# A new order of all steps in a layer of dilated window attention and gated MLP, with GpSimd's spreads of chunk 2 placed ahead of chunk 1's second norm

## The chip, the cores and the metric

The kernel runs on one core of a Trainium2 chip. The metric is the device time of one execution in microseconds (us), as the median of several. The engines have these names in the profile: PE is TensorE (matmuls; PEld its weight loads), DVE is VectorE, ACT is ScalarE, POOL is GpSimd and SP is SyncE, which only issues DMAs here. "L571" is line 571 of the kernel.

## What is computed

One block of a transformer over 2048 rows of 512 numbers in bfloat16. A layernorm, then attention with 32 heads of 16 in which each position sees itself and seven earlier ones at a distance of 2; then a second layernorm, and a gated MLP of width 1376 with a ReLU gate. Both halves add to their input.

```python
x = A_x
h = x + attention(_layernorm(x), A_wqkv, A_wo)     # W, dil = 8, 2; softmax over 8 offsets
n = _layernorm(h)
gate, up = n @ W_gate, n @ W_up
h2 = h + ((gate * (gate > 0)) * up) @ W_down
```

## The kernel before

The 2048 rows are worked in four chunks of 512, numbered 0 to 3 (`tk` in the code), and each chunk runs through the same steps.

- **First norm.** VectorE takes mean and variance (L492, L495), the rows are scaled (L548 to L553) and transposed, on TensorE with the identity (L582) or, for chunk 3, by a DMA transpose on SyncE's queue (L571).
- **q, k, v.** Twelve groups of four matmuls (L623), each written to one of the eight PSUM banks and copied out by ScalarE (L631).
- **Scores.** VectorE multiplies q with eight shifted copies of k (L674, in chunk 0 L689; L718 adds two products in some places), and TensorE sums over each head's numbers with the 0/1 matrix `sel` (L680, L732). There are two score groups for each chunk, for offsets 0 to 3 and 4 to 7 (`hf`), and ScalarE takes the exponential (L760). A sum of both halves goes through TensorE (L777) for the denominator, and VectorE multiplies each half with the reciprocal (L804).
- **Spreads.** The weights of a half lie on 32 partitions per offset. Four DMAs spread them to all 128 partitions (L820). A table, `BCD`, says which queue issues them: SyncE for most, GpSimd for the second half of chunk 2, the first half of chunk 3 and a part of chunk 0.
- **Weighted sum of v.** VectorE multiplies with shifted copies of v (L852, L867), half of the sum is done by accumulating DMAs that GpSimd issues (L895), and the rest by VectorE (L855, L859, L889).
- **Output projection and second norm.** Four groups of four matmuls (L933); VectorE adds the residual and sums the row (L944), centres it (L546; in chunk 0 ScalarE does it, L544), and SyncE transposes it by DMA (L571). The factor one over the standard deviation is applied only at the end. ScalarE sums the squares for it (L482).
- **MLP.** Gate and up groups of four matmuls (L1010), a narrow last one (L973), ReLU and copy on ScalarE (L1015, L1017, L1020), their product on VectorE (L1041; the narrow one L986 or L988, transposed by L996), then the down projection (L1064) and the output (L1070 or L1072). In chunks 0 and 1 the residual is added by an accumulating DMA of GpSimd (L1093).

What sets the order: each step is an operation with an engine, a planned duration, its dependences and its buffers. A planner goes through all 751 operations by a table of ranks, `RANK`, gives each the next free time of its engine, and the program is recorded in that order. So the table decides the order on every engine, and which of the buffers (five large ones of eight times 512, nine "quads" of transposed rows, eight banks) a step gets. Each engine works through its own row of instructions in that order and waits where an input isn't ready. SyncE's DMAs go out in their order as well. The two W_up loads (L317) wait for the attention of chunk 0, since their place is still used until then.

The operation of a spread is recorded like this; the line of its planned duration is the one that the change edits beside the table:

```python
abd.append(add(("bd%d%s" % (hf, eng[0]), tk), eng, len(ws) * BDI[eng[0]] + (0.35 if tk == 0 else 0), f_bd, [exd[hf]], apr + 1,
```

Of the kernel before, what the change touches and what calls it, by code (L numbers as in the profile page):

```python
# [15 lines left out]


RANK = [
# [38 lines left out]
]  # L57


# [34 lines left out]
class Plan:  # L94
# [9 lines left out]
    def add(self, key, *a, **k):  # L104
        op = Op(*a, **k)
        op.key = key
        op.seq = len(self.ops)
        if RANK:
            op.prio = RANK[op.seq]
        self.ops.append(op)  # L110
        for b in set(op.take) | set(op.use):
            b.left += 1
        return op
# [88 lines left out]
def kernel(  # L202
# [164 lines left out]
    add = plan.add  # L367
# [20 lines left out]
    BDI = {"S": 0.63, "A": 0.65, "P": 0.95}  # L388
# [217 lines left out]
    for tk in range(NCK):  # L606
# [48 lines left out]
        apr = base + 20  # L655
        exs, exd = [], []
# [3 lines left out]
        for hf in range(2):  # L660
            sc, ex = Buf(at_s), Buf(ex_s)
            scd, prd = [], []
            for t in range(0, NT, 2):
# [32 lines left out]
                else:  # L696
                    a = add(("pr%d" % hf, tk), "DVE", D40, f_pr, [d[k] for k in (t, t + 1) for d in (qd, kd, kp)],
                            apr, take=[pb], use=[qT], lat=DL)
# [110 lines left out]
        ab, abd = Buf(ab_s), []  # L809
        for w0 in range(0, W, BCN):  # L810
            hf = w0 // 4
            if (tk, hf) in BCD:
                for eng, q in (("SP", nc.sync), ("ACT", nc.scalar), ("POOL", nc.gpsimd)):
                    ws = [w for w in range(4) if BCD[tk, hf][w] == eng[0]]
                    if not ws:
                        continue

                    def f_bd(ws=ws, q=q, w0=w0, ab=ab, ex=exs[hf]):
                        for w in ws:
                            q.dma_start(ab.t[:, w0 + w, :], ex.t[w * HB:(w + 1) * HB, :].unsqueeze(1).to_broadcast([HB, 4, CS]))  # L820

                    abd.append(add(("bd%d%s" % (hf, eng[0]), tk), eng, len(ws) * BDI[eng[0]] + (0.35 if tk == 0 else 0), f_bd, [exd[hf]], apr + 1,
                                   take=[ab], use=[exs[hf]], lat=0.92 + ((-0.2 if hf == 0 else 0.6) if tk == 0 else 0),
                                   dq=(1.38 - BDI[eng[0]] * len(ws), 0.5 + BDI[eng[0]] * (len(ws) - 1))))
                continue
            bcs = [Buf(at_s) for _ in range(BCN)]

            def f_bc(w0=w0, bcs=bcs, ex=exs[hf]):
                for n, bc in enumerate(bcs):
                    r = (w0 + n) % 4 * HB  # L830
                    nc.tensor.matmul(bc.t[:], lhsT=spread[r:r + HB, :], rhs=ex.t[r:r + HB, :],
                                     start=True, stop=True, tile_position=(r, 0))

            a = add(("bc%d" % hf, tk), "PE", MM + SW, f_bc, [exd[hf]], apr + 1, take=bcs, use=[exs[hf]], lat=PEL)
            for n, bc in enumerate(bcs):
                def f_be(w=w0 + n, bc=bc, ab=ab):
                    nc.scalar.copy(out=ab.t[:, w, :], in_=bc.t[:])

                abd.append(add(("be%d" % hf, tk), "ACT", A5, f_be, [a], apr + 1, take=[ab], use=[bc], lat=AL))
# [120 lines left out]
        for f0 in range(0, NFT, 2):  # L960
# [42 lines left out]
            for ft in fts:  # L1003
# [31 lines left out]
                d = add(("ge%d" % (f0 // 2), tk), "ACT", A5, f_ge, [c], pr - 200, take=[gr], use=[gm], lat=AL)  # L1035
# [118 lines left out]
```

## Time and profile before

| what | value |
|---|---|
| median of 3 runs | 192.62 us (192.37 to 193.03) |
| profiled execution, its own time | 193.05 us |
| its span, from the first to the last instruction | 191.3 us |
| DMA transposes of the second norm (L571), chunk 1 | issued from 87.26 us, over 5.13 us |
| GpSimd's spreads (L820), chunk 2, second half | issued from 91.29 us, over 2.23 us |
| TensorE's wait ahead of chunk 1's MLP | 1.52 us, up to 95.72 us |

How to read it. A timeline row gives the start, the length, the engine, the line, the operation, what it writes and reads, and how many instructions were merged into it; behind it in brackets stands the idle time of the engine ahead of the row and what ended it. "SPq" rows are DMAs being issued; "DMA to landing" counts from the issue of a DMA to its last byte. A row of the waits is: engine and line, what it waited for, total, times, longest. In the chain of waits a row gives the start, the length and the step. By groups, a row gives busy time and the mean ns of one instruction behind the bar. A row of windows gives the stretch, its length, and the busy time of PE, PEld, DVE, ACT and POOL, each with a count, then the clock, the DMA share and GB/s.

### The profile page before, as it was taken

How to read it: one execution, taken by the hardware profiler on the slowest of the kernel's cores; microseconds unless marked ns; L12 is line 12 of the kernel's file. 1: busy time of each engine (PE TensorE's matmuls, PEld its weight loads, DVE VectorE, ACT ScalarE, POOL GpSimd, SP SyncE). 2: the span in 40 equal slices, each digit the busy share in tenths (PEclk: the TensorE clock that was granted, in tenths of full speed). 3: DMA queues.
4: the chain of work that ended last, by engine and by line, in shares of the span. 5: the costliest groups of instructions: out<-in, count | busy, mean ns of one | idle time of the engine just before them, and what ended most of it. 6: DMA issues, size and time to landing. Idle time of an engine off the chain costs nothing.

```text
span 191.3 us, 2948 instructions
## 1 busy us (share of the span) xinstructions
PE 183.1 (96%) x1058; PEld 92.3 (48%) x1077; DVE 149.3 (78%) x226; ACT 116.4 (61%) x241; POOL 25.1 (13%) x46
## 2 busy tenths in 40 slices
PE   7799998999999999999799999999999999999994
PEld 7555454554454435544244455444455446444453
DVE  6899989999999999999997979899382905022233
ACT  4579997986784585784428885132758612369600
POOL 3000403300000032100514214013300000000000
PEclk9999999999999999999999999999999999999999
DMA  5799384990598979862736899969930342201002
GB/s 183 267 326 386 76 206 94 194 202 17 178 209 188 280 167 188 153 137 55 160 63 124 165 192 213 152 151 178 179 54 3 92 100 82 55 3 55 0 24 86
DMA packets 27742, 26.96 MB, mean 141 GB/s; under 512 B 14704, under 2 KB 23248, under 8 KB 27728
## 3 DMA queue, kind: packets, MB, share of 16 engines
q1 hardware_dynamic: 23696, 15.47, 31.2%
q0 software_dynamic: 3312, 10.49, 28.5%
q10 hardware_dynamic: 720, 0.82, 1.3%
q8 instruction: 8, 0.13, 0.3%
q14 instruction: 6, 0.05, 0.1%
HBM read 8.42 MB, written 2.10 MB: 55 GB/s over the span
## 4 chain that ended last, share of the span: by engine, by line
PE 78%; DVE 8%; DMA 6%; ACT 4%; issue 2%; SPq 1%; DVEq 0%; ACTq 0%
PE bank L1010 35%; PE bank L1064 20%; PE bank L623 11%; PE bank L933 7%; DVE big L689 4%; DMA x_sm<-in_A_x_dram 3%; PE bank L973 3%; DMA big<-ex 3%; DVE st L492 2%; PE bank L680 2%; ACT up_sb L1015 1%; DVE big L867 1%; ACT quad L631 1%; PE bank L582 1%; PE bank L732 1%
## 5 line engine op out<-in xcount | busy, mean ns | idle before, releaser
L1010 PE MATMUL bank<-quad,wgu_sb 128*128 128x512 bf16 x312 | 70.6, 379 | 1.9 <-issue 1.5
L1010 PEld LDWEIGHTS <-wgu_sb 128*128 128x128 bf16 x320 | 30.9, 98 | 39.4 <-issue 3.3
L1064 PE MATMUL bank<-wd_sb,gT 128*128 128x512 bf16 (+3 forms) x195 | 39.1, 355 | 0.2
L623 PE MATMUL bank<-quad,wqk_sb 128*128 128x512 bf16 (+1 forms) x131 | 30.0, 370 | 0.6 <-DMA wqk_sb<-in_A_wqkv_dram 0.5
L1041 DVE TENSOR_TENSOR gT<-gr,up_sb 128x1024 bf16<-128x1024 bf16 x20 | 13.7, 690 | 20.7 <-ACT gr L1020 16.8
L1020 ACT ACTIVATE gr<-bank 128x512 bf16<-128x512 f32 x40 | 23.3, 605 | 9.0 <-PE bank L1010 9.0
L1064 PEld LDWEIGHTS <-gT 128*128 128x128 bf16 (+1 forms) x198 | 18.5, 98 | 19.4
L674 DVE TENSOR_TENSOR big<-quad,kT 128x4096 bf16<-128x4096 bf16 x11 | 25.0, 2285 | 0.0
L1017 ACT CAST up_sb<-bank 128x512 bf16<-128x512 f32 x30 | 17.1, 594 | 10.8 <-PE bank L1010 5.1
L623 PEld LDWEIGHTS <-wqk_sb 128*128 128x128 bf16 x134 | 14.7, 114 | 13.3 <-DMA wqk_sb<-in_A_wqkv_dram 1.1
L852 DVE TENSOR_TENSOR big<-big,vT 128x4096 bf16<-128x4096 bf16 x9 | 20.6, 2288 | 0.0
L482 ACT ACTIVATE junk<-x_sm,sm 128x512 bf16<-128x512 bf16 x17 | 12.3, 726 | 8.1 <-DVE x_sm L944 8.1
L623 PE MATMUL bank<-quad,wv_sb 128*128 128x512 bf16 x62 | 15.9, 379 | 0.1
L895 POOL DMA_DIRECT2D big<-big x13 | 11.2, 869 | 35.7 <-DVE big L852 25.5
L933 PE MATMUL bank<-wo_sb,quad 128*128 128x512 bf16 x61 | 14.5, 379 | 0.1
L1072 DVE SCALAR_TENSOR_TENSOR row<-bank,iv,x_sm 128x512 bf16<-128x512 f32 (+2 forms) x10 | 6.2, 641 | 10.6 <-issue 5.6
L855 DVE TENSOR_TENSOR big<-big 128x1024 bf16<-128x1024 bf16 (+1 forms) x17 | 10.4, 624 | 2.3 <-DMA big<-big 2.3
L820 POOL DMA_DIRECT2D big<-ex x12 | 6.8, 592 | 38.2 <-DVE st L492 19.0
L631 ACT CAST kT<-bank 128x512 bf16<-128x512 f32 x16 | 9.2, 592 | 4.0 <-PE bank L623 3.1
L944 DVE SCALAR_TENSOR_TENSOR x_sm<-x_sm,bank 128x512 bf16<-128x512 bf16 x16 | 10.7, 678 | 0.6 <-PE bank L933 0.6
L631 ACT CAST quad<-bank 128x512 bf16<-128x512 f32 x16 | 9.1, 590 | 2.7 <-PE bank L623 2.7
L492 DVE BATCH_NORM_STATS2 st<-x_sm 128x6 f32<-128x512 bf16 x15 | 9.7, 680 | 0.8 <-DMA x_sm<-in_A_x_dram 0.8
(84 smaller groups left out, 184.4 us busy)
## 6 DMA issues: line engine op xcount, KB each, us to landing
big<-big POOLq DMA_DIRECT2D x13, 512.0 KB, 5.0
big<-ex SPq DMA_DIRECT2D x20, 128.0 KB, 2.7
big<-ex POOLq DMA_DIRECT2D x12, 128.0 KB, 4.1
wgu_sb<-in_B_W_gate_dram SPq DMA_DIRECT2D x1, 1376.0 KB, 9.7
wgu_sb<-in_B_W_up_dram SPq DMA_DIRECT2D x2, 688.0 KB, 5.8
wd_sb<-in_B_W_down_dram SPq DMA_DIRECT2D x2, 640.0 KB, 5.5
x_sm<-in_A_x_dram SPq DMA_DIRECT2D x2, 512.0 KB, 6.4
wqk_sb<-wqk_sb POOLq DMA_DIRECT2D x2, 512.0 KB, 5.3
```

The source lines that it names most:

```text
L482: nc.scalar.activation(out=junk[:, j % 2, :], in_=h.t[:] if h else x_sm[:, tk * BPC + j, :], func=ACT.Square, bias=sm.t[:, j:j + 1], scale ...
L492: V.bn_stats(out=st.t[:], in_=x_sm[:, tk * BPC + j, :])
L623: nc.tensor.matmul(mm.t[:, lo:hi], lhsT=wv_sb[:, dt, t:D:NT] if c == 2 else wqk_sb[:, dt, c * D + t:(c + 1) * D:NT], rhs=xnT.t[:, dt, lo:h ...
L631: nc.scalar.copy(out=o, in_=mm.t[:])
L674: V.tensor_tensor(out=pb.t[:].rearrange("p (t w) s -> p t w s", t=2), in0=q4, in1=k4, op=ALU.mult)
L852: V.tensor_tensor(out=mt.t[:], in0=ab.t[:], in1=v8, op=ALU.mult)
L933: nc.tensor.matmul(od.t[:], lhsT=OT.t[:, t, j * P:(j + 1) * P], rhs=wo_sb[:, t, :], start=(t == 0), stop=(t == NT - 1 and tk not in RPE))
L1010: nc.tensor.matmul(mm.t[:fs, lo:hi], lhsT=wgu_sb[:, dt, g, ft * P: ft * P + fs], rhs=hnT.t[:, dt, lo:hi], start=(dt == 0), stop=(dt == NT ...
L1017: nc.scalar.copy(out=ub.t[:fs, i, :], in_=um.t[:fs, :])
L1020: nc.scalar.activation(out=gr.t[:fs, i, :], in_=gm.t[:fs, :], func=ACT.Relu, scale=-1.0 if tk in HX else 1.0)
L1041: V.tensor_tensor(out=gt.t[:fs, 0:n, :], in0=gr.t[:fs, 0:n, :], in1=ub.t[:fs, 0:n, :], op=ALU.mult)
L1064: nc.tensor.matmul(od.t[:, c0:c1], lhsT=gts[ft].t[:fs, ft % 2, j * P:(j + 1) * P], rhs=wd_sb[:fs, ft, c0:c1], start=(ft == 0), stop=(ft == ...
```

## The change

It edits two things. The table `RANK` is replaced: 751 other ranks. And the planned duration of GpSimd's spread of the first half in chunk 0 is raised from 0.35 to 0.85 above its base; this number enters the plan and no instruction.

```diff
 RANK = [
-    0, 1, 2, 3, 5, 6, 7, 8, 14, 15, 13, 12, 16, 17, 18, 19, 20, 21, 4, 9,
+    1, 0, 2, 3, 5, 8, 9, 11, 14, 15, 12, 13, 17, 16, 18, 19, 20, 21, 4, 7,
...
-                    abd.append(add(("bd%d%s" % (hf, eng[0]), tk), eng, len(ws) * BDI[eng[0]] + (0.35 if tk == 0 else 0), f_bd, [exd[hf]], apr + 1,
+                    abd.append(add(("bd%d%s" % (hf, eng[0]), tk), eng, len(ws) * BDI[eng[0]] + ((0.85 if eng=="POOL" and hf==0 else 0.35) if tk == 0 else 0), f_bd, [exd[hf]], apr + 1,
```

The instructions are the same in number and kind on every engine; only their order and their buffers differ. Three places follow. In each, the numbers behind a name are those of the buffers, and they differ between the two orders without a meaning of their own.

**VectorE, second norm of chunk 1, before.** `ex` is the weights of a half of chunk 2, `x_sm` the rows with the residual, `row` the centred rows.

```order
L944 SCALAR_TENSOR_TENSOR x_sm,sm_123<-x_sm,bank_140 128x512
L1041 TENSOR_TENSOR gT_98<-gr_111,up_sb_109 128x1024
L546 TENSOR_SCALAR row_108<-x_sm,sm_123 128x512
L804 TENSOR_TENSOR ex_101<-ex_101,rec_103 128x512
L718 TENSOR_TENSOR big_91<-big_91,wqk_sb 128x4096
```

The multiply L804, on whose result GpSimd's spreads of chunk 2 wait, stands behind the last of the four L546.

**VectorE, the same place now**, from that multiply to the first residual addition L944 of chunk 1.

```order
L804 TENSOR_TENSOR ex_100<-ex_100,rec_103 128x512
L674 TENSOR_TENSOR big_88<-quad_87,kT 128x4096
L986 SCALAR_TENSOR_TENSOR row_108<-gr_112,bank_144 128x2x96
L855 TENSOR_TENSOR big_91<-big_91 128x1024
L855 TENSOR_TENSOR big_92<-big_92 128x1024
L889 TENSOR_TENSOR quad_79<-big_91 128x512
L889 TENSOR_TENSOR quad_79<-big_92 128x512
L674 TENSOR_TENSOR big_89<-quad_87,kT 128x4096
L944 SCALAR_TENSOR_TENSOR x_sm,sm_123<-x_sm,bank_140 128x512
L546 TENSOR_SCALAR row_105<-x_sm,sm_123 128x512
```

It has moved ahead of all four L944 and L546. GpSimd's own row keeps the four spreads at the same place, behind the four accumulating DMAs of chunk 1.

**SyncE, second norm of chunk 0, before**, from the loads of W_up to the first spreads of chunk 1.

```order
L317 DMA wgu_sb<-in_B_W_up_dram 128x2x1376 x2
L571 DMA_TRANSPOSE quad_80<-row_106 128x4x128
L571 DMA_TRANSPOSE quad_80<-row_107 128x4x128
L571 DMA_TRANSPOSE quad_80<-row_104 128x4x128
L571 DMA_TRANSPOSE quad_80<-row_105 128x4x128
L820 DMA big_89<-ex_100 128x1x512 x4
```

**SyncE, the same place now.**

```order
L317 DMA wgu_sb<-in_B_W_up_dram 128x2x1376
L571 DMA_TRANSPOSE quad_80<-row_106 128x4x128
L317 DMA wgu_sb<-in_B_W_up_dram 128x2x1376
L571 DMA_TRANSPOSE quad_80<-row_105 128x4x128
L571 DMA_TRANSPOSE quad_80<-row_107 128x4x128
L571 DMA_TRANSPOSE quad_80<-row_104 128x4x128
L820 DMA big_90<-ex_100 128x1x512 x4
```

The first transpose now goes out between the two loads.

**TensorE, ahead of the second score group of chunk 1, before.** Two rows, a weight load and a matmul, stand for each matmul; the last matmul and the first of the scores are shown.

```order
L623 MATMUL bank_146<-quad_84,wqk_sb 128x512
L933 LDWEIGHTS quad_85
L933 MATMUL bank_147<-wo_sb,quad_85 128x512
...
L680 LDWEIGHTS sel
L680 MATMUL bank_145<-big_90,sel 32x512
```

**TensorE, the same place now.**

```order
L933 MATMUL bank_143<-wo_sb,quad_85 128x512
L933 LDWEIGHTS quad_85
L933 MATMUL bank_142<-wo_sb,quad_85 128x512
...
L680 LDWEIGHTS sel
L680 MATMUL bank_144<-big_88,sel 32x512
```

In both orders the first score group of chunk 1 begins at row 609 of TensorE. The second begins at row 705 before and at row 697 now: between the two groups stand 32 matmuls before (eight groups of four) and 28 now (seven). The first gate or up matmul of chunk 1 is at row 1174 in both, so that the four matmuls now stand behind the scores. The first L1010 of chunk 0 is at row 795 before and 787 now.

In chunk 2, VectorE's product L852 that stood behind the gate product L1041 stands ahead of it now.

74 rows, old and new, of the table RANK are left out of this document.

## The prediction

> **What bounds the kernel now.** I read the page first: busy time by engine, the granted clock, the shares of the chain.
>
> ```profile
> span 191.3 us, 2948 instructions
> PE 183.1 (96%) x1058; PEld 92.3 (48%) x1077; DVE 149.3 (78%) x226; ACT 116.4 (61%) x241; POOL 25.1 (13%) x46
> PEclk9999999999999999999999999999999999999999
> PE 78%; DVE 8%; DMA 6%; ACT 4%; issue 2%; SPq 1%; DVEq 0%; ACTq 0%
> ```
>
> TensorE is busy nearly all the time at full clock, and nothing in the change removes a matmul. A new order can therefore gain only what TensorE now waits, and the next view is the list of TensorE's waits; then its timeline at the longest of them.
>
> ```profile
> PE bank L1010 <- issue: 1.5, 1, 1.5
> PE bank L582 <- ACT row L548: 0.5, 1, 0.5
> ```
>
> ```profile
> 88.63 5.57 PE L1064 MATMUL bank<-wd_sb,gT 128*128 128x512 bf16 x25
> 95.72 3.61 PE L1010 MATMUL bank<-quad,wgu_sb 128*128 128x512 bf16 x16 [1.52 <-issue]
> ```
>
> The one long wait is 1.52 us before 95.72, at the first gate or up matmul (L1010) of chunk 1. That matmul needs the four DMA transposes of the chunk's second norm (L571). Two windows on L571, and what GpSimd and VectorE did beside them, show why it is late:
>
> ```profile
> 87.26 5.13 SPq L571 DMA_TRANSPOSE quad<-row  x4
> L571 SPq DMA_TRANSPOSE quad<-row x2: 1210/1213/1216, 88.6 to 89.9; - x2
> DMA to landing us min/median/max: 2.4/2.4/2.4
> ...
> L571 SPq DMA_TRANSPOSE quad<-row x1: 1229/1229/1229, 91.2 to 91.2; - x1
> DMA to landing us min/median/max: 4.5/4.5/4.5
> ...
> 90.57 0.42 DVE L804 TENSOR_TENSOR ex<-ex,rec 128x512 bf16<-128x512 bf16 x1
> 91.29 2.23 POOL L820 DMA_DIRECT2D big<-ex  x4 [14.29 <-DVE ex L804]
> ```
>
> The middle transposes land 2.4 us after issue. The fourth, issued at 91.2, takes 4.5 us and lands at 91.2 + 4.5 = 95.7, which is when TensorE starts. GpSimd's four spreads (L820) went out at 91.29, released by the multiply L804 at 90.57. At 2.4 us it would have landed at 93.6, before TensorE ran dry at 95.72 - 1.52 = 94.20.
>
> **Term 1: the spreads leave the transposes.** In the new order that multiply stands before the residual additions L944 of chunk 1. Its time follows by counting back from the first L944.
>
> ```profile
> 83.92 2.29 DVE L674 TENSOR_TENSOR wqk_sb<-quad,kT 128x4096 bf16<-128x4096 bf16 x1
> 86.12 0.68 DVE L944 SCALAR_TENSOR_TENSOR x_sm<-x_sm,bank 128x512 bf16<-128x512 bf16 x1
> ...
> L855 DVE TENSOR_TENSOR big<-big 128x1024 bf16<-128x1024 bf16 (+1 forms) x17 | 10.4, 624 | 2.3 <-DMA big<-big 2.3
> L889 DVE TENSOR_TENSOR quad<-big 128x512 bf16<-128x512 bf16 x9 | 3.5, 423 | 0.1
> L986 DVE SCALAR_TENSOR_TENSOR row<-gr,bank 128x192 bf16<-128x192 bf16 x2 | 0.7, 354 | 0.0
> ```
>
> Ahead of that L944 stands the same VectorE work as before plus this one multiply, so it moves from 86.12 to about 86.5. Back from there stand two L674 (2 x 2.29), two L855 (2 x 0.62), two L889 (2 x 0.42), one L986 (0.35) and the multiply (0.42): 7.4 us, so it starts at about 79.1. GpSimd follows 0.72 us later (91.29 - 90.57) and issues for 2.23 us, from 79.8 to 82.0; even 4.5 us to landing ends at 86.5. The first transpose goes out at 87.26 + 0.4 = 87.7, the fourth at 91.6, landing at 94.0, which is before 94.20. Term 1 is **-1.52 us**. Its bounds are 0 (the transpose stays at 4.5 us) and -1.52: no more than the wait can go.
>
> [...]
>
> **Term 2: TensorE has less to do before the scores of chunk 1.** The second score group (L680) of chunk 1 needs VectorE's products (L674).
>
> ```profile
> 43.54 1.05 PE L680 MATMUL bank<-big,sel 128*32 128x512 bf16 x16
> ...
> 50.75 0.65 PE bank L933 x3
> 51.40 0.15 issue
> 51.55 1.05 PE bank L680 x16
> ...
> 49.10 2.27 DVE L674 TENSOR_TENSOR big<-quad,kT 128x4096 bf16<-128x4096 bf16 x1
> ```
>
> The product ends at 49.10 + 2.27 = 51.37 and TensorE begins its scores at 51.55 after only 0.15 us at rest: it comes just in time. VectorE's rows up to that product are the same number and kinds in both orders, so the product stays at 51.4. On TensorE the first score group stands at the same row in both, but between the two groups there are 28 matmuls instead of 32; the missing four stand later, between these scores and the first L1010 of chunk 1, which is again at the same row. Four matmuls at the chain's pace (L1010 x30 in 6.65 us, so 0.22 each) are 0.88 us. TensorE then waits 0.88 + 0.15 for the scores instead of 0.15, unless it is already late by then. Whatever was won or lost before 51 us is absorbed by this wait.
>
> ```profile
> 60.11 6.65 PE bank L1010 x30
> ```
>
> What is behind the scores is longer by those four matmuls, so TensorE reaches the place of the old gap later: 0.88 less the 0.15 that it rested there already, **+0.73 us**. The bounds are 0 (TensorE comes late and fills this wait) and 0.88. It would arrive there at 94.20 + 0.73 = 94.93, and the fourth transpose landed at 94.0; so nothing of term 1 is lost.
>
> The 0.5 us wait at L582 (31 to 33 us) may also go, since the new order puts chunk 3's q block there. It lies before the scores of chunk 1, so I cost it at nothing: that wait covers it.
>
> **Term 3: the loads of W_up among the transposes of chunk 0.** SyncE's queue now takes one transpose between the two loads.
>
> ```profile
> 48.61 1.60 SPq L317 DMA_DIRECT2D wgu_sb<-in_B_W_up_dram  x2
> 50.31 6.26 SPq L571 DMA_TRANSPOSE quad<-row  x4
> ...
> L317 SPq DMA_DIRECT2D wgu_sb<-in_B_W_up_dram x1: 392/392/392, 48.6 to 48.6; - x1
> DMA to landing us min/median/max: 4.1/4.1/4.1
> ...
> L317 SPq DMA_DIRECT2D wgu_sb<-in_B_W_up_dram x1: 1156/1156/1156, 49.1 to 49.1; - x1
> DMA to landing us min/median/max: 7.4/7.4/7.4
> ...
> L571 SPq DMA_TRANSPOSE quad<-row x1: 1217/1217/1217, 55.4 to 55.4; - x1
> DMA to landing us min/median/max: 3.1/3.1/3.1
> ...
> 58.81 9.66 PE L1010 MATMUL bank<-quad,wgu_sb 128*128 128x512 bf16 x43
> ```
>
> The second load ended at 49.1 + 7.4 = 56.5, the last transpose at 55.4 + 3.1 = 58.5, and TensorE's first L1010 began at 58.81. After the change it wants to begin at 58.81 - 0.88 + 0.73 = 58.66. If the load and the transposes use the queue as fully as before, the last transpose lands at 58.5 again: cost 0. If the load takes 7.4 us from its new issue (after a transpose, at about 50 + 1.3 = 51.3), it ends at 58.7, and the three transposes behind it at 0.5 us each (four landed in the 2.0 us from 56.5 to 58.5) at 60.2; the cost is up to 60.2 - 58.7 = 1.5. I take **0**, because the first load landed early enough (4.1 us from 48.61) for the second one's data to follow without a pause. [...] No run here shows the second order yet.
>
> **Term 4: later pacing points.** In chunk 2 TensorE's L933 depend on VectorE's sums:
>
> ```profile
> 118.27 0.42 DVE L889 TENSOR_TENSOR quad<-big 128x512 bf16<-128x512 bf16 x1
> 119.06 3.62 PE L933 MATMUL bank<-wo_sb,quad 128*128 128x512 bf16 x16
> ...
> 110.00:120.00 10.00, 9.95 (x57) 5.29 (x57) 8.40 (x17) 6.79 (x16) 3.07 (x5) 1.00 0.97 206
> ```
>
> The last sum ends at 118.69 and L933 begins at 119.06: 0.37 us of slack. With TensorE 0.79 us earlier, L933 wants to begin at 118.27, so VectorE must be 0.42 us earlier too. It rests 1.6 us of these ten, and in the new order a large product (L852) stands ahead of the gate product (L1041) that it waited for. I take 0; the bound is +0.42 us. The last stage has the same output pieces in the same sizes, and TensorE has no wait there in either: 0.
>
> **The sum**: -1.52 + 0.73 + 0 + 0 = -0.79 us. The profiled run took 193.05 us (1.8 us around its span of 191.3) and gives 192.26; it lies 0.43 above the median of 192.62, so the median becomes 192.62 - 0.79 = **191.8 us**. About 0.3%, 0.58 us, is what a measurement of this kernel can tell from no change: faster means below 192.04, slower above 193.20.
>
> **Rivals.**
> - *The whole wait is won*: TensorE arrives late at the scores, term 2 vanishes. 192.62 - 1.52 = 191.1. For it: waits early in the kernel could make it late. Against it: 0.15 us of rest shows it early. Chance 0.12.
> - *The gain is taken back at the next pacing point* (term 4): 191.8 + 0.4 = 192.2, more with a second such point, 192.5 at most. Chance 0.20.
> - *The change doesn't do what it says*: some other transfer lengthens the fourth transpose to 4.5 us, so it lands at 91.6 + 4.5 = 96.1, 0.4 us later than now: 193.0. Against it: the next DMA behind the spreads on GpSimd is L1093, which waits for the last sums of chunk 0's output and went out at 95.21. Chance 0.06.
>
> ```profile
> 95.21 0.91 POOL L1093 DMA_DIRECT2D x_sm<-up_sb  x1 [1.69 <-ACT up_sb L1070]
> ```
>
> - *Slower*: term 3 at its upper bound, 191.8 + 1.5 = 193.3. It decides if the second W_up load lands after about 57.2 (58.7 less the 1.5 us of three transposes). For it: 7.4 us is what that load took. Chance 0.20.
>
> My forecast has 0.42. The range from 191.0 to 193.3 takes all of these in; the forecast's own is 191.4 to 192.1. Faster: 0.12 and 0.38 of the forecast, 0.50. Slower: the last rival, 0.20. The rest, 0.30, is within 0.3%.
>
> **What would show it.** In the new profile: no wait of 1.5 us ahead of L1010 near 94 us, L820 on GpSimd near 80 us, four transposes at about 2.4 us (term 1); a rest of about 1 us ahead of L680 near 51 us (term 2); L1010 of chunk 0 beginning by 58.8 (term 3); L933 of chunk 2 near 118.3 without a wait (term 4). Wrong would be: TensorE's waits not summing to some 0.8 us less than before, or a new wait on DMA ahead of the first L1010.

## The result and the profile after

The changed kernel takes 191.15 us in the median of 7 runs (190.84 to 192.01), the kernel before, on the same chip, 192.37 us (7 runs). The ratio is 0.994, with a 95% interval from 0.992 to 0.997: 1.2 us faster, where 0.8 was forecast. Of the 36 executions of b_two_early, b_two_early_stats and b_spread_later below, ten took at least 1.5% longer than the fastest of their kernel; ratios and medians leave these out, but the one profile of b_two_early_stats is of such an execution (194.06 us, mean granted clock 0.991).

From the profile of the changed kernel, the page's head and its chain of waits, the list of TensorE's waits, and TensorE's and VectorE's timelines:

```profile
span 189.0 us, 2973 instructions
PE 94%; ACT 3%; ACTq 1%; issue 0%; DVE 0%
```

```profile
PE bank L437 <- DVE warm L329: 1.0, 1, 1.0
PE bank L582 <- DVE row L553: 1.0, 1, 1.0
PE bank L582 <- ACT row L548: 0.5, 1, 0.5
```

```profile
50.15 1.05 PE L680 MATMUL bank<-big,sel 128*32 128x512 bf16 x16
...
57.41 1.46 PE L1010 MATMUL bank<-quad,wgu_sb 128*128 128x512 bf16 x6
...
93.50 3.83 PE L1010 MATMUL bank<-quad,wgu_sb 128*128 128x512 bf16 x17
...
47.62 2.27 DVE L674 TENSOR_TENSOR big<-quad,kT 128x4096 bf16<-128x4096 bf16 x1
```

The wait ahead of L1010 is gone from the list, and all that is listed lies before 20 us. The chain that ended last is now TensorE to 94% (78% before). Three steps of the prediction can be read off here: L1010 of chunk 1 begins at 93.50 without a wait, L1010 of chunk 0 at 57.41 without a wait, and the second score group of chunk 1 at 50.15, with no wait either, though one of about 1 us was forecast. VectorE's last product for it ends at 47.62 + 2.27 = 49.89, not at 51.4.

SyncE's third and fourth transpose of chunk 1's second norm, and GpSimd's four spreads, by line and window:

```profile
L571 SPq DMA_TRANSPOSE quad<-row x2: 1216/1216/1217, 88.9 to 90.2; - x2
DMA to landing us min/median/max: 2.4/2.5/2.5
...
L820 POOL DMA_DIRECT2D big<-ex x4: 567/589/599, 79.0 to 80.6; - x4
DMA to landing us min/median/max: 4.1/4.5/4.9
```

The spreads leave at 79.0 to 80.6 (79.8 to 82.0 forecast) and the fourth transpose lands after 2.5 us instead of 4.5.

One profile is one execution, and the two differ in more than the change: the load that opens the q and k weights landed at 7.64 us in the one of before and at 6.70 us in this one, with the same issue time of 1.66 us. So I cut each profile where TensorE passes the same two places: the start of the second score group (L680) of chunk 1 and the first L1010 of chunk 1. The table holds all kernels of the study; names beginning with b stand for the order of before and those with a for the changed one. The stretches are differences of the start times in the timelines and of the span, in us.

| kernel | start to scores | scores to L1010 | L1010 to end |
|---|---|---|---|
| before | 51.55 | 44.17 | 95.6 |
| b_again | 51.27 | 44.14 | 95.5 |
| changed | 50.15 | 43.35 | 95.5 |
| a_again | 50.92 | 43.36 | 95.5 |
| b_spread_early | 50.54 | 42.54 | 96.1 |
| a_spread_late | 50.84 | 44.20 | 99.0 |
| b_early_four | 51.12 | 43.71 | 95.6 |
| b_two_early | 51.43 | 42.54 | 96.0 |
| b_two_early_stats | 50.23 | 42.54 | 99.4 |
| a_load_first | 50.73 | 43.36 | 95.5 |
| b_spread_sync | 50.90 | 42.49 | 95.9 |
| b_early_stats | 51.10 | 42.60 | 95.9 |
| a_three_rows | 50.28 | 43.36 | 95.6 |
| b_spread_later | 50.94 | 42.50 | 96.9 |

The middle stretch and the last come out alike in two profiles of one kernel (44.17 and 44.14, 43.35 and 43.36); luck lies in the first. Before to changed the middle falls by 0.82 us, the last by nothing, and the first by 1.40 between these two profiles but 0.35 between the second pair.

### The profile page after: what moved, and what is told of

Its sections match the earlier page's. It is cut to its first block, busy times and chain, and to the rows that moved or that the text cites. A ratio compares the mean times of both kernels' runs of the same rounds, so it can differ in the third digit from the quotient of the medians.

```text
span 189.0 us, 2973 instructions
## 1 busy us (share of the span) xinstructions
PE 183.6 (97%) x1077; PEld 92.3 (49%) x1077; DVE 149.3 (79%) x226; ACT 116.9 (62%) x241; POOL 25.1 (13%) x46
## 4 chain that ended last, share of the span: by engine, by line
PE 94%; ACT 3%; ACTq 1%; issue 0%; DVE 0%
PE bank L1010 37%; PE bank L623 22%; PE bank L1064 20%; PE bank L933 7%; PE bank L973 3%; PE bank L680 3%; PE bank L582 1%; PE bank L732 1%; ACT L328 1%; ACT quad L598 1%; ACTq L327 0%; ACTq L325 0%; PE bank L777 0%; ACT row L548 0%; ACT junk L482 0%; ACT rs L508 0%
## 5 line engine op out<-in xcount | busy, mean ns | idle before, releaser
L1010 PE MATMUL bank<-quad,wgu_sb 128*128 128x512 bf16 x320 | 72.4, 379 | 0.0
L1010 PEld LDWEIGHTS <-wgu_sb 128*128 128x128 bf16 x320 | 31.0, 98 | 37.1 <-issue 1.3
L1064 PE MATMUL bank<-wd_sb,gT 128*128 128x512 bf16 (+3 forms) x198 | 39.6, 355 | 0.0
L674 DVE TENSOR_TENSOR big<-quad,kT 128x4096 bf16<-128x4096 bf16 x11 | 25.1, 2286 | 0.0
L852 DVE TENSOR_TENSOR big<-big,vT 128x4096 bf16<-128x4096 bf16 x11 | 24.7, 2289 | 0.0
L1041 DVE TENSOR_TENSOR gT<-gr,up_sb 128x1024 bf16<-128x1024 bf16 x20 | 13.6, 689 | 9.4 <-ACT gr L1020 6.3
L895 POOL DMA_DIRECT2D big<-big x14 | 12.4, 883 | 64.5 <-DVE big L852 55.0
L933 PE MATMUL bank<-wo_sb,quad 128*128 128x512 bf16 x64 | 14.8, 379 | 0.0
L855 DVE TENSOR_TENSOR big<-big 128x1024 bf16<-128x1024 bf16 (+2 forms) x20 | 12.9, 662 | 1.8 <-DMA big<-big 1.7
L944 DVE SCALAR_TENSOR_TENSOR x_sm<-x_sm,bank 128x512 bf16<-128x512 bf16 x16 | 10.7, 679 | 2.7 <-PE bank L933 2.7
L623 PEld LDWEIGHTS <-wv_sb 128*128 128x128 bf16 x64 | 6.9, 114 | 7.1 <-issue 1.3
L820 POOL DMA_DIRECT2D big<-ex x12 | 6.8, 591 | 23.8 <-DVE st L492 18.3
```

Source lines behind the costliest of these rows:

```text
L623: nc.tensor.matmul(mm.t[:, lo:hi], lhsT=wv_sb[:, dt, t:D:NT] if c == 2 else wqk_sb[:, dt, c * D + t:(c + 1) * D:NT], rhs=xnT.t[:, dt, lo:h ...
L674: V.tensor_tensor(out=pb.t[:].rearrange("p (t w) s -> p t w s", t=2), in0=q4, in1=k4, op=ALU.mult)
L852: V.tensor_tensor(out=mt.t[:], in0=ab.t[:], in1=v8, op=ALU.mult)
L855: V.tensor_tensor(out=mt.t[:, 0:n, :], in0=mt.t[:, 0:n, :], in1=mt.t[:, n:2 * n, :], op=ALU.add)
L895: nc.gpsimd.dma_start(mt.t[:, 0:4, :], mt.t[:, 4:8, :], accum_op=ALU.add)
L933: nc.tensor.matmul(od.t[:], lhsT=OT.t[:, t, j * P:(j + 1) * P], rhs=wo_sb[:, t, :], start=(t == 0), stop=(t == NT - 1 and tk not in RPE))
```

## The experiments

All of them edit the order alone, by moving steps in the table of ranks, but for b_spread_sync. Each diff shows rows of one engine; where a moved step also changes the names of buffers, that is left out. Ratios are against the kernel before.

### What one profile varies by

Both kernels once more, without an edit.

> The kernel before, unchanged, to see what one profile of it may vary by. Theory A (the gap of 2.3 us between the two profiled spans, 191.3 and 189.0, is mostly the change): ratio 1.000, and again VectorE waits some 0.8 us before the first L867 of chunk 0 (27 us) and TensorE 1.5 to 1.9 us before the first L1010 of chunk 1 (94 us). Rival B (part of that gap is luck of one execution): the wait of 1.5 to 1.9 us is there again, but the first loads land up to 0.9 us earlier and the wait before L867 is shorter or gone.

> The changed kernel, unchanged. Theory A: VectorE again has no wait before the first L867 and TensorE no wait before the second L680 of chunk 1 nor before L1010 of chunk 1; about 191.2 us. Rival B: the first loads land later by up to 0.9 us or VectorE waits up to 0.8 us before the first L867, and then TensorE waits up to 0.7 us before the second L680 of chunk 1 (near 51 us); such an execution takes about 191.9 us.

b_again took 192.63 us, ratio 1.000 (0.998 to 1.002); a_again 191.42 us, ratio 0.993 (0.990 to 0.995). From the timelines of VectorE, ScalarE and TensorE in b_again:

```profile
27.10 1.23 DVE L867 TENSOR_TENSOR big<-big,vT 128x2048 bf16<-128x2048 bf16 x1 [1.01 <-DMA big<-ex]
...
29.58 0.30 ACT L508 ACTIVATE rs<-mv,eps_t 128x4 f32<-128x4 f32 x1 [1.33 <-DVE mv L495]
...
32.77 0.40 PE L582 MATMUL bank<-identity,row 128*128 128x128 bf16 x4 [0.69 <-ACT row L548]
...
95.41 1.89 PE L1010 MATMUL bank<-quad,wgu_sb 128*128 128x512 bf16 x8 [1.49 <-issue]
```

The wait ahead of L1010 is the same as in the first profile (1.49 and 1.52). The loads landed early this time (6.56 us), and in a_again late (7.54 us): so that part of the 2.3 us between the first two spans was luck, as rival B said. The wait ahead of the first L867 of chunk 0 came back, 1.01 us, and the rows show what hangs on it: L495 stands behind it on VectorE, ScalarE waits for that, and TensorE for ScalarE's rows. In a_again neither VectorE nor TensorE waited there.

### Term 1 alone, forward and back

In b_spread_early the one multiply is moved in the kernel before; in a_spread_late it is moved back in the changed kernel.

```diff
 L804 TENSOR_TENSOR ex_100<-ex_100,rec_103 128x512
 L986 SCALAR_TENSOR_TENSOR row_106<-gr_112,bank_141 128x2x96
+L804 TENSOR_TENSOR ex_101<-ex_101,rec_103 128x512
...
-L804 TENSOR_TENSOR ex_101<-ex_101,rec_103 128x512
 L718 TENSOR_TENSOR big_91<-big_91,wqk_sb 128x4096
```

```diff
-L804 TENSOR_TENSOR ex_100<-ex_100,rec_103 128x512
 L674 TENSOR_TENSOR big_88<-quad_87,kT 128x4096
...
+L804 TENSOR_TENSOR ex_100<-ex_100,rec_103 128x512
 L674 TENSOR_TENSOR wqk_sb<-quad_87,kT 128x4096
 L852 TENSOR_TENSOR big_91<-big_90,vT 128x4096
```

> The kernel before, with one step moved alone: VectorE's L804 of chunk 2, second half, stands right behind L986 that follows the first half's L804, so GpSimd's four spreads go out near 81 us instead of 91.3. Theory (term 1: these spreads lengthen the fourth transpose): the four transposes L571 of chunk 1 land after about 2.4 us each, the wait of 1.5 to 1.9 us before chunk 1's first L1010 is gone, and the kernel takes 1.4 to 1.8 us less than before, ratio 0.991 to 0.993; all else as before. Rival (the wait is VectorE's or the new order's as a whole): the fourth transpose takes 4.5 us again or the wait stays, ratio 1.000.

> The changed kernel, with L804 of chunk 2, second half, and its four spreads on GpSimd put back behind the last L546 of chunk 1's second norm, as in the kernel before. Theory (term 1): the spreads go out near 90 us, the fourth transpose takes about 4.5 us, TensorE waits 1 to 1.9 us before the first L1010 of chunk 1, and the kernel takes as long as before or 0.4 us less, ratio 0.998 to 1.003. Rival (the other parts of the new order remove the wait): no wait, about 191.2 us, ratio 0.994.

b_spread_early took 191.13 us, ratio 0.992 (0.990 to 0.995): 1.47 us less than before, and no more than the changed kernel. TensorE's timeline has no wait at chunk 1's L1010, and a new one in chunk 2:

```profile
93.08 4.26 PE L1010 MATMUL bank<-quad,wgu_sb 128*128 128x512 bf16 x19
...
126.56 3.18 PE L1010 MATMUL bank<-quad,wgu_sb 128*128 128x512 bf16 x14 [0.35 <-DMA quad<-row]
```

In the table the middle falls by 1.6 us and the last stretch grows by 0.5 to 0.6. Together that is -1.1; where the other 0.4 us of the medians lie, one profile can't show. One step out of 751 brings the whole gain in time.

a_spread_late took 194.01 us, ratio 1.008 (1.005 to 1.011): not the time of before, as the theory had it, but more: 2.6 us slower than a_again. The fourth transpose, TensorE's wait at chunk 1's L1010, and three waits of VectorE and TensorE that neither theory had:

```profile
L571 SPq DMA_TRANSPOSE quad<-row x1: 1227/1227/1227, 90.8 to 90.8; - x1
DMA to landing us min/median/max: 4.1/4.1/4.1
...
95.04 3.18 PE L1010 MATMUL bank<-quad,wgu_sb 128*128 128x512 bf16 x14 [0.68 <-issue]
...
96.03 2.29 DVE L852 TENSOR_TENSOR big<-big,vT 128x4096 bf16<-128x4096 bf16 x1 [3.20 <-DMA big<-ex]
...
110.62 0.38 PE L777 MATMUL bank<-row,same 128*128 128x512 bf16 x1 [1.39 <-ACT gr L1020]
131.32 1.89 PE L1010 MATMUL bank<-quad,wgu_sb 128*128 128x512 bf16 x8 [1.46 <-DMA quad<-row]
```

The transpose is slow again (4.1 us), so the theory on it holds; the wait that it causes is 0.68 us, less than the 1 to 1.9 expected. This execution took 195.78 us, 1.8 more than the kernel's median, so the waits behind it need not be typical in size. And the changed kernel has its first L852 of chunk 2 already at 91.83, in front of other large products, and this L852 reads the spreads: with the multiply put back, VectorE stands 3.2 us, and TensorE waits 1.39 us at 110 us and 1.46 us at 131 us. The new order can't do without the early spreads, which no row of before could show.

### Term 2: four matmuls fewer

```diff
 L680 MATMUL x16
 L623 MATMUL x8
-L623 MATMUL x4
 L933 MATMUL x12
 L623 MATMUL x4
 L933 MATMUL x4
 L680 MATMUL x16
+L623 MATMUL x4
```

> b_spread_early with one more move: one block of four matmuls L623 that stood ahead of the second score group (L680) of chunk 1 stands behind it, so TensorE has 28 instead of 32 matmuls there, as in the changed kernel, while VectorE's order stays that of before. Theory (term 2: VectorE's last L674 of that group sets the time): TensorE is done 0.86 us earlier than VectorE allows; it rests 0.5 to 0.9 us ahead of L680 and the kernel takes 0.5 to 0.8 us more than b_spread_early (191.6 to 191.9 us). Rival (VectorE is well ahead there in any order): no rest beyond the 0.10 us that every profile shows at this change of lines, and the time of b_spread_early (191.1).

It took 191.85 us, ratio 0.997 (0.995 to 0.999), against 0.992 for b_spread_early: 0.7 to 0.8 us slower, about the amount that the theory gave. From the timelines of VectorE and TensorE, and the line's own view (the starts of the group's first and last matmul in it):

```profile
49.53 2.27 DVE L674 TENSOR_TENSOR big<-quad,kT 128x4096 bf16<-128x4096 bf16 x1
...
51.12 1.36 PE L680 MATMUL bank<-big,sel 128*32 128x512 bf16 x16
...
L680 PE MATMUL bank<-big,sel x16: 376/379/390, 51.1 to 52.1; 128*32 128x512 bf16 x16
```

TensorE begins the group at 51.12, before the product ends at 51.80, and the 16 matmuls take 1.36 us instead of the 1.05 in every other profile: it rests 0.31 us inside the group, not 0.5 to 0.9 ahead of it. The first eight matmuls use the product before; only the other eight need the last. So VectorE had more room than the forecast gave it, and the rest explains 0.31 us of the 0.7 to 0.8. This profile also has a wait of 0.99 us ahead of the first L867, which that of b_spread_early lacks; what the remainder is was not shown. In this profile the middle stretch is 1.17 us longer than in b_spread_early: the four matmuls (0.86) and this rest.

### Term 3: the two loads

```diff
+L317 DMA wgu_sb<-in_B_W_up_dram 128x2x1376 x2
-L317 DMA wgu_sb<-in_B_W_up_dram 128x2x1376
 L571 DMA_TRANSPOSE quad_80<-row_106 128x4x128
-L317 DMA wgu_sb<-in_B_W_up_dram 128x2x1376
 L571 DMA_TRANSPOSE quad_80<-row_105 128x4x128
```

> The changed kernel with SyncE's two loads L317 of chunk 0 next to each other again, ahead of the four transposes L571, as before. Theory (term 3 at 0: the queue's total counts, not the order): the last of the four transposes lands at the same time within 0.3 us, TensorE's first L1010 of chunk 0 begins without a wait, and the time is that of the changed kernel, ratio 0.992 to 0.995. Rival (a pause between the loads costs): the transposes land up to 1.5 us earlier or later than in the changed kernel and the time changes by more than 0.3 us.

191.03 us, ratio 0.993 (0.991 to 0.995), and in the table the stretches of the changed kernel. The order of the loads costs nothing either way.

### The same bytes on another queue, and later

b_spread_sync edits the table of queues in the kernel before; b_spread_later moves the multiply one large operation later, and one L852 out of the way.

```diff
-(2,1):"PPPP"
+(2,1):"SSSS"
```

```diff
+L718 TENSOR_TENSOR big_91<-big_91,wqk_sb 128x4096
 L804 TENSOR_TENSOR ex_101<-ex_101,rec_103 128x512
-L718 TENSOR_TENSOR big_91<-big_91,wqk_sb 128x4096
 L674 TENSOR_TENSOR big_88<-quad_86,kT 128x4096
 L674 TENSOR_TENSOR big_92<-quad_86,kT 128x4096
+L718 TENSOR_TENSOR big_88<-big_88,big_92 128x4096
 L852 TENSOR_TENSOR big_90<-big_89,vT 128x4096
-L718 TENSOR_TENSOR big_88<-big_88,big_92 128x4096
```

> The kernel before, in its own order, with the four spreads of chunk 2, second half, issued by SyncE behind the four transposes L571 instead of by GpSimd. The same bytes start at nearly the same time (the first at some 92.5 us instead of 91.3). Theory (the fourth transpose is slowed by spreads on another queue while it is under way): it takes 2.4 to 2.9 us and lands near 93.6 us instead of 95.6, TensorE waits less than 0.4 us instead of 1.5 to 1.9 before chunk 1's first L1010, and the time is 1.3 to 1.7 us below that of before (ratio 0.991 to 0.994). Rival (the spreads' traffic near 92 to 95 us slows the transpose whichever queue they are on): it takes over 3.5 us, the wait stays above 1 us, ratio 0.997 to 1.001.

> The kernel before with VectorE's L804 of chunk 2, second half, put one L718 (2.2 us) later instead of earlier, and, so that nothing waits for its spreads, the first L852 of chunk 2 behind the second L718 of chunk 3. GpSimd's spreads then go out near 93.2 us, some 2.3 us after SyncE began to issue the fourth transpose, instead of 0.13 us after it. Theory (only a GpSimd transfer issued within some 0.5 us of the transpose slows it): the fourth transpose takes 2.4 to 2.6 us and lands near 93.3 us, and TensorE waits less than 0.4 us before chunk 1's first L1010, as in b_spread_early, though the spreads come later and not earlier; the time is 0.5 to 1.5 us below that of before, ratio 0.992 to 0.997. Rival (the spreads have to be out of the way early): the transpose takes over 3 us or the wait of 1.5 us stays, ratio 0.999 or more.

In both, the view of L571 gives 2.4 to 2.5 us to landing, and TensorE's timeline begins L1010 without a wait; here b_spread_sync:

```profile
L571 SPq DMA_TRANSPOSE quad<-row x2: 1216/1216/1217, 89.2 to 90.5; - x2
DMA to landing us min/median/max: 2.4/2.5/2.5
...
93.39 2.97 PE L1010 MATMUL bank<-quad,wgu_sb 128*128 128x512 bf16 x13
```

So it isn't enough that the spreads' traffic falls near 92 to 95 us. With the spreads issued by SyncE at 91.8, behind the transpose on its own queue, or by GpSimd 2.3 us behind its issue, the transpose is as fast as ever. The times didn't follow: 192.05 us, ratio 0.998 (0.995 to 1.000), and 193.0 us, ratio 1.004 (1.001 to 1.008). The profiled executions took 191.11 and 192.12 us, 0.8 to 0.9 us less than these medians, so the profiles don't show where that part goes. In the profile of b_spread_later the last stretch is 1.4 us longer than before, with small waits at 117 us for VectorE's sums and at 123 us for L996's transpose; its L852 and everything behind it came later.

### Looking for more

Three tries at what was left. b_two_early and b_two_early_stats build on b_spread_early, b_early_stats is the latter without the former's move, a_three_rows is the changed kernel.

```diff
 L804 TENSOR_TENSOR ex_100<-ex_100,rec_103 128x512
+L804 TENSOR_TENSOR ex_102<-ex_102,rec_103 128x512
...
-L804 TENSOR_TENSOR ex_102<-ex_102,rec_103 128x512
```

```diff
+L495 BN_AGGR mv_120<-st_115 128x2
 L867 TENSOR_TENSOR x2
-L495 BN_AGGR mv_120<-st_115 128x2
 L867 TENSOR_TENSOR
+L516 SCALAR_TENSOR_TENSOR nb_129<-mv_120,rs_134 128x4
 L867 TENSOR_TENSOR
-L516 SCALAR_TENSOR_TENSOR nb_129<-mv_120,rs_134 128x4
```

```diff
-L582 MATMUL bank_140<-identity,row_105 128x128 x4
 L582 MATMUL bank_147<-identity,row_108 128x128 x4
 L582 MATMUL bank_140<-identity,row_104 128x128 x4
+L623 MATMUL x4
+L582 MATMUL bank_147<-identity,row_105 128x128 x4
 L680 MATMUL x16
-L623 MATMUL x4
```

> b_spread_early with one more move: VectorE's L804 of chunk 3, first half, stands right behind that of the second half, so GpSimd's four spreads of chunk 3 go out near 110.5 us instead of 113.7. Theory (the same collision again: with these spreads in flight L996's transpose took 5.75 us and held up SyncE's queue, and TensorE waited 0.35 us before chunk 2's first L1010): the transpose takes about 4.0 us or less, TensorE does not wait at chunk 2's first L1010 (126 to 127 us), and the kernel takes 0.3 to 0.5 us less than b_spread_early, some 190.7 us. Rival (those 0.35 us are SyncE's own queue: L1096 and L996 ahead of the transposes): the wait stays, 191.1 us.

> b_two_early with two more moves on VectorE: the last L495 of chunk 2's first norm stands ahead of the first L867 instead of behind the second, and its L516 one L867 earlier. Theory (the chain in the two profiles of before: the first L867 waits 0.8 to 1.0 us for a spread, L495 waits behind it, ScalarE waits 1.1 to 1.3 us for L495, TensorE waits 0.5 to 0.7 us for ScalarE's L548 at L582 near 32.5 us): ScalarE's wait and TensorE's at 32.5 us are gone also in an execution whose spread lands late, and the median falls by 0.2 to 0.6 us against b_two_early. Rival (the late spread alone decides): VectorE's wait comes back as often and the median stays.

> b_spread_early with two VectorE moves of b_two_early_stats only: the last L495 of chunk 2's first norm ahead of the first L867, its L516 one L867 earlier; the spreads of chunk 3 stay where they were. Theory (chain late spread, L867, L495, ScalarE, TensorE's L582): TensorE has no wait near 32.5 us even if the first L867 waits, and the median is 0.2 to 0.6 us below b_spread_early, 190.5 to 190.9 us. Rival: the late spread costs as much elsewhere (TensorE rests at a later score group), 191.1 us.

> The changed kernel with TensorE's L582 of chunk 1 in the order in which ScalarE writes their rows (the third-written one was first) and a block of four L623 ahead of the third. Theory (in the changed kernel TensorE waits 0.5 us for ScalarE's L548 near 17 us, with two rows long ready): the wait is gone, and as VectorE has 0.3 us or more to spare at the later score groups, the time falls by 0.3 to 0.5 us, to 190.8 us or so. Rival (VectorE's last L689 of chunk 0, which ends at 20.0 us, sets the second score group anyway): TensorE rests at L680 instead and the time stays at 191.3 us.

b_two_early took 192.5 us, ratio 1.000 (0.998 to 1.003): worse than b_spread_early by 1.4 us. L996's transpose did fall from 5.75 to 3.16 us, but the wait in chunk 2 stayed (0.33 us at L1010), and with it the theory fell. b_two_early_stats took 192.3 us, ratio 0.998 (0.996 to 1.000). Its profile shows the wait in chunk 2 grown, and something behind it; the windows of stretches give the granted clock in the third column from the right:

```profile
127.87 5.30 PE L1010 MATMUL bank<-quad,wgu_sb 128*128 128x512 bf16 x16 [2.09 <-DMA quad<-row]
...
L571 SPq DMA_TRANSPOSE quad<-row x1: 1219/1219/1219, 123.8 to 123.8; - x1
DMA to landing us min/median/max: 3.9/3.9/3.9
...
123.85 0.91 POOL L895 DMA_DIRECT2D big<-big  x1 [11.12 <-DMA quad<-row]
...
122.00:125.00 3.00, 3.00 (x16) 1.33 (x15) 3.00 (x2) 0.69 (x1) 0.91 (x1) 1.00 0.43 88
128.00:129.00 1.00, 1.00 (x5) 0.43 (x4) 1.00 (x2) 0.00 (x0) 0.76 (x1) 0.84 0.95 268
129.00:132.00 3.00, 3.00 (x8) 1.03 (x7) 2.29 (x2) 0.60 (x1) 0.52 (x2) 0.50 1.10 204
```

It looks like the same collision one chunk on. Here another GpSimd transfer, an accumulating DMA (L895), was issued at 123.85, right behind SyncE's fourth transpose at 123.8, which took 3.9 us. TensorE waited 2.09 us, and then ran at half clock from 129 to 132 us. It is one execution, 1.8 us above its kernel's median, so it doesn't tell what the median lost. Bringing GpSimd forward does bring L895 closer to that transpose: 0.55 to 0.79 us behind it in b_spread_early, b_two_early, b_early_four and b_early_stats, 1.44 us in before and 0.92 us in b_again.

b_early_stats took 191.60 us, ratio 0.995 (0.992 to 0.998), not better than b_spread_early. ScalarE no longer waits for L495, though the first L867 did wait 0.68 us; TensorE then rests 0.4 us at an L680 for L674. That is as the rival said: VectorE's late products cost the time, wherever they are waited for. a_three_rows took 191.16 us, ratio 0.993 (0.991 to 0.995), no gain either, for its own rival's reason; TensorE's timeline:

```profile
19.50 0.40 PE L680 MATMUL bank<-big,sel 128*32 128x512 bf16 x4
20.18 0.83 PE L680 MATMUL bank<-big,sel 128*32 128x512 bf16 x12 [0.28 <-DVE big L689]
```

The 0.5 us at L582 is gone and turns in part into a rest for VectorE's L689. No version beat the changed kernel beyond the intervals.

## Why the prediction was right, and the step that was not

**Term 1 (-1.52 us): right**, in mechanism and size. The fourth transpose fell from 4.5 to 2.5 us; the multiply alone gave -1.47 us (b_spread_early). The three profiles with the spreads right behind the transpose (before, b_again, a_spread_late) have it at 4.1 to 4.5 us; putting them earlier, later or on SyncE's queue gives 2.5. The collision did not vanish, though: it moved to a transpose that TensorE doesn't wait for. L996's transpose of chunk 0's narrow product, in the changed kernel and then before:

```profile
L996 SPq DMA_TRANSPOSE gT<-row x1: 2572/2572/2572, 81.2 to 81.2; - x1
DMA to landing us min/median/max: 4.8/4.8/4.8
...
L996 SPq DMA_TRANSPOSE gT<-row x1: 1298/1298/1298, 83.1 to 83.1; - x1
DMA to landing us min/median/max: 2.7/2.7/2.7
```

It took 4.6 to 5.2 us in the nine profiles in which GpSimd had issued the four spreads 0.5 to 2.2 us ahead of it, and 2.5 to 2.8 us in the other five. GpSimd issued the four as soon behind the multiply as before (0.72 us after its start, in both), at 567 to 599 ns each from 79.0 us, beside a 2.29 us L674 of VectorE that had begun at 78.64.

**Term 2 (+0.73 us): the step that failed.** It said that VectorE's product sets the start of the scores and stays at 51.4, so that TensorE's wait there takes up whatever came before. The sum for the middle stretch came out, -1.52 + 0.73 = -0.79 against -0.82 measured. What was wrong is the start of that stretch: it was to stay, and it came earlier by 1.40 and 0.35 us in the two pairs. Over the profiles whose early order is untouched, the scores begin at 51.1 on average in the order of before (six: 51.55, 51.27, 50.54, 51.43, 50.90, 50.94) and at 50.7 in the new one (four: 50.15, 50.92, 50.84, 50.73). That alone shows little, since the single starts scatter by 0.8 to 1.0 us.

The scatter is smaller from chunk 0's first score group on, between which and chunk 1's second one TensorE has 197 matmuls in both orders. That stretch is 32.9 to 33.1 us long in five of the six of before, in which VectorE waited 0.64 to 1.01 us ahead of the first L867 and TensorE then 0.45 to 0.69 us at L582 near 33 us. It is 32.2 to 32.4 us long in the sixth, b_spread_early, where neither waited, and in the four of the new order, where neither did at these places (a_load_first waited 0.34 us ahead of its third L867). So the wait at L582 is the term that was mis-sized: the prediction said that it may go and costed it at nothing, as covered by the wait for the scores, and it was worth some 0.6 us. With -0.82 that makes -1.4; the medians gave -1.2 here and in a_again and -1.55 in a_load_first, so the sizes agree to some 0.2 us and no better. In the new order that L582 also stands eight matmuls further behind chunk 0's scores, and the changed kernel passes it without a wait:

```profile
33.38 0.61 PE L582 MATMUL bank<-identity,row 128*128 128x128 bf16 x8
```

Two readings led me wrong. The first is the 0.15 us at rest ahead of L680. The rows there, of before and of b_again:

```profile
50.59 0.81 PE L933 MATMUL bank<-wo_sb,quad 128*128 128x512 bf16 x3
...
50.31 1.03 PE L933 MATMUL bank<-wo_sb,quad 128*128 128x512 bf16 x4
51.27 1.05 PE L680 MATMUL bank<-big,sel 128*32 128x512 bf16 x16
```

The L933 come in groups of four, and in the profile of before one of the four has no record: the rest is its place. In b_again, where all four are there, the last ends behind the start of L680, and TensorE didn't rest at all; in b_spread_early it comes to L680 just as closely, though VectorE's product was done 0.3 us before. So TensorE set the start of the scores already before the change. The second reading is that the whole group needs the last product, where its first eight matmuls do not: b_early_four shows 0.31 us of rest for the missing 0.86. And VectorE itself did not stay, as the wait ahead of the first L867 is in none of the four.

What that wait of VectorE hangs on was not settled. It ends when GpSimd's second spread of chunk 0 lands, and that spread took 4.75 to 5.11 us in the five profiles and 3.84 in the sixth, against 3.42 to 3.62 in the four, issued at the same distance from its neighbours. That the new order is the reason is likely; how was not found.

**Term 3 (0): right.** L1010 of chunk 0 began without a wait, at 57.41, the two loads landed 4.7 to 5.5 us after their issue (4.1 and 7.4 before), and a_load_first, at 191.03 us against 191.15, shows no difference between the two orders of loads. **Term 4 (0): right.** The stretch behind L1010 is 95.5 us in both.

**Of the rivals**, the whole wait won (191.1) came closest, in its number and in its condition: TensorE came to the scores 0.2 to 0.3 us after VectorE's product in three of the four profiles of the new order. It had been given a chance of 0.12, because of the 0.15 us at rest, which was none. The slower one, term 3 at 193.3, had no part in it.

A thing the forecast did not see is what the rest of the new order is for. It brings no time over b_spread_early, but it keeps SyncE's fourth transpose and GpSimd's next transfer apart in chunk 2 as well: 1.67 us in the changed kernel (1.44 in before), 0.58 in b_spread_early, 0.06 in the one profile of b_two_early_stats. Whether the longer times of the b kernels come from there was not shown.

## What to carry to other kernels

Where an engine waits for a transfer that took longer than its neighbours, look at the issue times on the other queues before you look at the engine; here moving one step on the engine that releases the other transfer was enough. Before you take a short rest for a wait, count the instructions ahead of it, compare the end of the supposed releaser with the row ahead on the engine itself, and look at a second profile. A wait early in the kernel may be costed at nothing only if a later one is shown to cover it. And look for the next place with the same two neighbours, since what comes earlier here arrives earlier there.

## What the runs showed of the hardware

For the fourth transposes of the second norm in chunks 1 and 2, how far behind them GpSimd's next transfer is issued goes with the time that they take. The transfer is the spreads (L820) at 90 to 93 us and L895 at 123 to 129 us. From the times of issue and landing in the traces:

| profile | transpose issued | GpSimd's next issued | apart | transpose took |
|---|---|---|---|---|
| b_two_early_stats | 123.79 | 123.85 | 0.06 | 3.95 |
| before | 91.16 | 91.29 | 0.13 | 4.47 |
| a_spread_late | 90.80 | 90.93 | 0.13 | 4.15 |
| a_spread_late | 127.97 | 128.30 | 0.33 | 3.23 |
| b_spread_early | 123.72 | 124.30 | 0.58 | 2.70 |
| b_early_stats | 124.34 | 125.06 | 0.72 | 2.46 |
| changed | 123.28 | 124.95 | 1.67 | 2.44 |
| b_spread_later | 90.56 | 92.89 | 2.33 | 2.50 |

In these rows nothing is lost beyond some 0.7 us, and at 0.1 us it is 1.5 to 2 us. The distance is not the whole: near 30 us, in six profiles of the order of before, the fourth transpose of chunk 3's first norm took 3.0 to 3.1 us with L895 as much as 1.6 to 2.0 us behind it, and why was not found. Nor is the other side free, as L996's 4.6 to 5.2 us with the spreads ahead of it show. In b_spread_sync the same bytes on the transpose's own queue, the first of them issued 1.3 us behind it (91.8 against 90.5), cost it nothing: it took 2.5 us. How so small a distance comes to matter was not shown.

In the profile of b_two_early_stats a wait of 2.09 us on TensorE was followed by 3 us at a granted clock of 0.50, while the wait of 1.52 us in before left it at 1.00 from 95.72 to 100 us, and b_again, with 1.49 us, had a mean of 0.999 over its execution.

```profile
PEclk9999999999999999999999999987999999999999
```

This row is from the page of b_two_early_stats: the dip to 8 and 7 in the 27th and 28th of its 40 slices (4.8 us each, 125 to 134.5 us) is that stretch. This is one execution, and that the wait brought the lower clock is not shown.
